# A second group of the last batch's weights in attention's buffers, and the projection's factors behind their group's last product

## The chip, the core and the metric

The kernel runs on one core of a Trainium2 chip. Its time is device microseconds of one execution, of which the median of three runs is given. The engines are called as in the profile: PE is the matrix engine (PEld its weight loads), DVE the vector engine, ACT the scalar engine, POOL the general engine, SP the one that here only issues transfers. Each engine takes its instructions in its own order; an instruction whose input or output buffer is not ready holds up all behind it on that engine.

## The reference

Sliding-window attention with a distance bias, then a maxout layer with an output projection, all in float32. Cut to what is computed:

```python
# q, k, v: 8 batches x 8 heads x 576 positions x 64
scores = scale * np.matmul(q, k.transpose(0, 1, 3, 2))
bias = slopes[:, None, None] * (-np.abs(rel).astype(np.float32))[None, :, :]
mask = (rel >= 0) & (rel < window)            # window = 128
scores = np.where(mask, scores + bias[None], -1000000000.0)
scores = scores - np.max(scores, axis=-1, keepdims=True)
attn = np.exp(scores)
attn = attn / (np.sum(attn, axis=-1, keepdims=True) + 1e-09)
out = np.matmul(attn, v)
# x: the heads side by side, 4608 tokens x 512; w1, w2, w3: 512 x 768; w_out: 768 x 512
h = np.maximum(np.maximum(x @ w1, x @ w2), x @ w3)
return h @ w_out
```

## The kernel before, in words

**Two pipelines in one program.** For each of the eight batches there is attention (four head pairs, 36 steps of 128 queries or less) and then the maxout layer. Attention of batch b+1 runs between the maxout products of batch b. The last batch has no attention to run beside it.

**The maxout layer by units.** A batch's layer is 11 groups of 7 products, 77 *units*. Groups 0 to 8 are the gates: three blocks p of hidden features, and for each block the three weight matrices w = 0, 1, 2, so that p and w are the group's number divided by 3 and the rest. Groups 9 and 10 are the output projection. A group computes four quarters of a tile from seven half-size products (a Strassen scheme: seven products of sums and differences of quarters in place of eight), and each float32 product is made of three products of a high and a low part. So one gate product is 6 matmuls of 128x128 weights with 288 columns, and a group is 42. The seven products stand in the order k = 0, 1, (6 of the group before), 2, 3, 4, 5. Three of PSUM's banks (`ps_m0` to `ps_m2`) take turns: k = 0, 1 and 4 open one each, the others add to an open one. ACT copies the sums after k = 0, 1, 2 aside (L663), and `put` (L596) takes each finished quarter out of its bank: on DVE with L617/L618 or L612 where it is compared with the maximum so far, L620 and ACT's L614 for the first of the three matrices. The last quarter, (1, 0), comes from k = 6, so its take-out (L612) is in the middle of the next group, and the bank that it frees is the one that the next group's k = 4 opens.

**The factors of the projection.** When the third matrix of a block is done, the block's four quarters (`hq`) are the projection's input, and `factors_h` (L562) makes the seven factors from them: differences on DVE (`sub`, L531), and for each factor a high part on ACT (L527) and a low part on DVE (L528), into `hs`. They are put on a list with a unit's number (`later`, L519), and a unit first calls what is due by its number. For the blocks p = 0 and 1 the factors are needed only in groups 9 and 10, for p = 2 right away.

**The weights.** The nine gate groups' factors are made once, in the first batch, and kept in HBM (`keep`, two halves for each group: k = 0 to 3, 1024 KB, and k = 4 to 6, 768 KB). From then on each group's halves are loaded again by transfers that POOL issues (`stream`, L273, one call in each unit), into a ring of two tiles for each half (`wt`). A half is loaded when the product that reads it last in the group two before has been issued. In the last batch group 2 goes elsewhere: `SPARE` is its number in the whole run, and `spare` (L230) loads its seven pieces into buffers that attention no longer needs, as soon as the last batch's layer has begun (`begun == B`). The groups after it then find the ring free one group earlier.

**What sets the order.** All calls are sorted by a time written out by hand (`at`, L672), in steps of attention. The framework's scheduler then orders each engine's instructions by its own estimate; from the third batch of attention on, PE is held to the written order (`fix`).

```python
 ps = part_of[n, {2: 0, 5: 0, 6: 0, 3: 1}.get(k, k)]
 if w == 2:
     factors_h(b, p, ij, when + 1)
```

Of the kernel before, what the change touches and what calls it, by code (L numbers as in the profile page):

```python
# [24 lines left out]
RING = 2  # L25
# [7 lines left out]
def attention_maxout_kernel(  # L33
# [11 lines left out]
    nc = tc.nc  # L45
# [177 lines left out]
    SPARE = 9 * (B - 1) + 2  # L223

    def ahead(n, a):
        if n == SPARE:
            return begun == B
        return n < RING or (n - RING - (SPARE < n <= SPARE + RING), 6 if a else 3) in used

    def spare(n, a):  # L230
        for k in range(4 - a):
            w = (pp_p if a == 0 else s_p if k < 2 else v_p).tile(
                [P, 2, W], F32R, name="pp" if a == 0 else "pr" if k < 2 else "v", **({"bufs": 2} if a and k < 2 else {})
            )
            nc.gpsimd.dma_start(w, keep[n % 9][a][:, k])
            wts[n, a, k] = w

# [35 lines left out]
    def stream():  # L273
        nonlocal streamed
        n, a = divmod(streamed, 2)
        if n < 9 * B and prepared == 72 and ahead(n, a):
            streamed += 1
            if n == SPARE:
                return spare(n, a)
            place(n, a)  # L280
            nc.gpsimd.dma_start(wts[n, a], keep[n % 9][a])  # L281
# [237 lines left out]
    def later(when, what, *args):  # L519
        todo.append((when, what, args))  # L520
        todo.sort(key=lambda x: x[0])
# [40 lines left out]
    def factors_h(b, p, ij, when):  # L562
        b00, b01, b10, b11 = [hq.get((p, x)) for x in ((0, 0), (0, 1), (1, 0), (1, 1))]

# [11 lines left out]
        if ij == (0, 0):  # L576
# [3 lines left out]
            later(when, cut, 0, b00)  # L580
            later(when, cut, 1, t)
        elif ij == (1, 1):
            t = hq["t2", p]
            later(when, sub, t, b11, hq["t1", p])
            later(when, sub, b01, b11, b01)
            later(when, cut, 2, t)
            later(when, cut, 3, b11)
        elif ij == (1, 0):
            t = hq["t2", p]
            later(when, cut, 5, b01)  # L590
            later(when, cut, 4, b10)
            when += 2
            later(when, sub, t, b10, t)
            later(when, cut, 6, t)
# [31 lines left out]
    def unit(u):  # L626
# [9 lines left out]
        if g < 9:  # L636
            at = b * 9 + g
            if b == 0:
                weights(1.3, 6 * g_order.index(g) + 3 + (2, 2, 3, 3, 1, 2, 1)[k])
            wt, x = wts[at, k // 4][:, k % 4] if at != SPARE else wts[at, k // 4, k % 4], xs[b, k]  # L640
            pairs = [
                (wt[:, a, kt * P:(kt + 1) * P], x[:, c, kt]) for kt in range(2) for a, c in ((0, 1), (1, 0), (0, 0))
# [135 lines left out]
```

## Time and profile before

| what | value |
|---|---|
| time, median of 3 runs | 781.05 us (779.34 to 781.97) |
| profiled execution | 781.4 us, of which the span of its instructions 779.7 us |
| PE busy | 750.3 us, 96% of the span |
| DVE busy | 554.6 us, 71% |
| ACT busy | 520.8 us, 67% |
| POOL busy | 188.1 us, 24% |
| read from HBM, written | 157.74 MB, 25.95 MB |

A group's row in the profile has the line, the engine, the operation, the tile written and the tiles read, the shape and the count, then busy time and the mean of one. In a table of waits a row says which engine sat idle at which line, for whose work it waited, the sum, the number of times and the longest. In a timeline a row has start, length, engine, line, tiles and count, and in brackets the idle time before it with what ended it. Line numbers are those of the kernel before.

### The profile page before, as it was taken

How to read it: one execution, taken by the hardware profiler on the slowest of the kernel's cores; microseconds unless marked ns; L12 is line 12 of the kernel's file. 1: busy time of each engine (PE TensorE's matmuls, PEld its weight loads, DVE VectorE, ACT ScalarE, POOL GpSimd, SP SyncE). 2: the span in 40 equal slices, each digit the busy share in tenths (PEclk: the TensorE clock that was granted, in tenths of full speed). 3: DMA queues.
4: the chain of work that ended last, by engine and by line, in shares of the span. 5: the costliest groups of instructions: out<-in, count | busy, mean ns of one | idle time of the engine just before them, and what ended most of it. 6: DMA issues, size and time to landing. Idle time of an engine off the chain costs nothing.

```text
span 779.7 us, 19483 instructions
## 1 busy us (share of the span) xinstructions
PE 750.3 (96%) x7291; PEld 684.6 (88%) x7291; DVE 554.6 (71%) x1722; ACT 520.8 (67%) x1684; POOL 188.1 (24%) x393
## 2 busy tenths in 40 slices
PE   7888999999999999999999999999999999999997
PEld 3556878889998999999999998999999998999987
DVE  5888889885767847694777747794777747683662
ACT  6898787776767756776677766776677666542341
POOL 5331223211232122221222122221222122421100
PEclk9999999999999999999999999999999999999999
DMA  6862668594887559873888568974887567876651
GB/s 243 300 248 73 252 236 322 199 305 140 275 311 264 174 199 297 299 275 125 278 295 282 172 217 290 307 258 136 284 290 272 170 229 261 282 268 201 225 173 61
DMA packets 42398, 184.95 MB, mean 237 GB/s; under 512 B 4672, under 2 KB 13632, under 8 KB 33216
## 3 DMA queue, kind: packets, MB, share of 16 engines
q0 software_dynamic: 18864, 115.61, 44.1%
q1 hardware_dynamic: 23296, 67.97, 24.5%
q8 instruction: 57, 0.93, 0.5%
q14 instruction: 37, 0.30, 0.1%
q10 hardware_dynamic: 144, 0.13, 0.1%
HBM read 157.74 MB, written 25.95 MB: 236 GB/s over the span
## 4 chain that ended last, share of the span: by engine, by line
PE 64%; DVE 16%; ACT 8%; issue 7%; DMA 3%; POOL 1%; SPq 0%; POOLq 0%; DVEq 0%; ACTq 0%
PE ps_m L654 47%; PE ps_s L345 4%; PE pt L413 4%; PE ps_x L480 4%; DVE hs L528 3%; ACT p L386 2%; DVE hq L618 2%; DVE t L617 2%; PE pt L191 2%; DVE t L531 2%; DMA qk<-in_qk 1%; DMA hs<-in_w_all 1%; PE ps_m L191 1%; DMA wt<-keep 1%; DVE s L374 1%
## 5 line engine op out<-in xcount | busy, mean ns | idle before, releaser
L654 PE MATMUL ps_m<-xs,wt 128*128 128x288 f32 x2982 | 425.0, 298 | 10.4 <-DVE hq L612 3.6
L654 PEld LDWEIGHTS ps_m<-xs,wt 128*128 128x128 f32 x2982 | 402.8, 189 | 18.0 <-DVE hq L612 5.2
L663 ACT COPY t<-ps_m 128x288 f32<-128x288 f32 x264 | 103.3, 395 | 81.7 <-PE ps_m L654 79.0
L654 PE MATMUL ps_m<-hs,ow 128*128 128x288 f32 x1008 | 141.1, 297 | 3.4 <-DVE hs L528 1.6
L654 PEld LDWEIGHTS ps_m<-hs,ow 128*128 128x128 f32 x1008 | 134.4, 188 | 6.5 <-ACT t L663 2.6
L433 POOL TENSOR_SCALAR_AFFINE_SELECT pp<-pr 128x256 f32<-128x256 f32 x112 | 54.2, 484 | 313.1 <-ACT pr L417 183.2
L386 ACT ACTIVATE p<-s,st 128x128 f32<-128x128 f32 x288 | 115.1, 403 | 17.2 <-DVE st L374 14.5
L281 POOL DMA_DIRECT2D wt<-keep x124 | 66.9, 539 | 205.2 <-PE ps_m L654 199.5
L405 ACT ACTIVATE p<-p,st 128x128 f32<-128x128 f32 x252 | 85.4, 395 | 23.8 <-DVE st L393 23.5
L617 DVE TENSOR_TENSOR t<-ps_m,t 128x288 f32<-128x288 f32 x144 | 64.9, 453 | 48.1 <-PE ps_m L654 30.2
L374 DVE CUSTOM_DVE_ANT_0 s<-ps_s,bias 128x128 f32<-128x128 f32 x240 | 60.9, 286 | 11.8 <-POOL bias L116 4.7
L618 DVE TENSOR_TENSOR hq<-t,hq 128x288 f32<-128x288 f32 x144 | 65.5, 460 | 2.6
L345 PE MATMUL ps_s<-qk 64*64 64x192 f32 (+1 forms) x1088 | 63.4, 317 | 2.1 <-DMA qk<-in_qk 1.4
L527 ACT CAST hs<-hq 128x288 fp32r<-128x288 f32 x96 | 41.1, 434 | 23.3 <-DVE hq L618 20.6
L386 ACT ACTIVATION_READ_ACCUMULATOR p<-s,st 128x1 f32 x288 | 56.0, 195 | 0.0
L480 PE MATMUL ps_x<-pp,v 64*64 64x64 f32 (+3 forms) x1456 | 55.2, 274 | 0.0
L514 DVE TENSOR_TENSOR xk<-ps_x,xk 128x256 f32<-128x256 f32 (+3 forms) x56 | 25.5, 454 | 41.8 <-ACT xk L513 41.8
L480 PEld LDWEIGHTS ps_x<-pp,v 64*64 64x64 f32 x1456 | 42.3, 133 | 10.8 <-issue 9.2
L413 PE MATMUL pt<-plus,p 128*128 128x128 f32 x288 | 47.5, 286 | 1.5 <-POOL p L400 0.6
L437 POOL TENSOR_SCALAR_AFFINE_SELECT pp<-pr 128x256 f32<-128x256 f32 (+1 forms) x112 | 48.6, 434 | 1.1
L345 PEld LDWEIGHTS ps_s<-qk 64*64 64x64 f32 x1088 | 40.0, 134 | 9.3 <-issue 3.9
L413 PEld LDWEIGHTS pt<-plus,p 128*128 128x128 f32 x288 | 30.2, 140 | 19.8 <-issue 12.6
(98 smaller groups left out, 816.2 us busy)
## 6 DMA issues: line engine op xcount, KB each, us to landing
wt<-keep POOLq DMA_DIRECT2D x62, 1024.0 KB, 7.3
wt<-keep POOLq DMA_DIRECT2D x62, 768.0 KB, 5.9
qk<-in_qk SPq DMA_DIRECT2D x31, 576.0 KB, 5.3
hs<-in_w_all SPq DMA_DIRECT2D x12, 1023.6 KB, 7.0
v<-in_v SPq DMA_DIRECT2D x32, 320.0 KB, 5.8
keep<-wt SPq DMA_DIRECT2D x9, 1024.0 KB, 5.6
outT<-t SPq DMA_DIRECT2D x64, 144.0 KB, 1.8
keep<-wt SPq DMA_DIRECT2D x9, 768.0 KB, 4.6
```

The costliest lines, as they stand in the source:

```text
L281: nc.gpsimd.dma_start(wts[n, a], keep[n % 9][a])
L345: pe(nc.tensor.matmul(ps[j][d:d + D, o:o + k1 - k0], lhsT=qkt[u][j * D:(j + 1) * D, 0, q0:q0 + D], rhs=qkt[u][j * D:(j + 1) * D, 1, k0:k1] ...
L374: nc.vector.tensor_tensor_reduce(out=x, in0=ps[j][:, P:2 * P], in1=below, scale=-0.125, scalar=3.0e38, op0=ALU.add, op1=ALU.min, accum_out ...
L386: nc.scalar.activation(p[:, j], x, AF.Exp, bias=st[:, 0, a, j:j + 1], scale=-1.0, accum_out=st[:, 1, a, j:j + 1])
L405: nc.scalar.activation(p[:, j], p[:, j], AF.Copy, scale=st[:, 2, a, j:j + 1])
L413: pe(nc.tensor.transpose(out=pt[:, a, j], in_=p[:, j], identity=ident))
L433: nc.gpsimd.affine_select(out=old, in_=src, pattern=[[-x, n] for x, n in pat], compare_op=ALU.is_gt, fill=0.0, base=0, channel_multiplier=1,)
L480: pe(nc.tensor.matmul(x[j * D:(j + 1) * D, r, o:o + rhs.shape[1]], lhsT=vv[k, i, j * D:(j + 1) * D], rhs=rhs[k], start=start, stop=True, s ...
L617: nc.vector.tensor_tensor(out=s, in0=ps, in1=e, op=ALU.add)
L618: nc.vector.tensor_tensor(out=h, in0=s, in1=h, op=ALU.max)
L654: pe(nc.tensor.matmul(ps, lhsT=lt, rhs=rt, start=i == 0 and k in (0, 1, 4), stop=i == len(pairs) - 1, skip_group_check=True,))
L663: nc.scalar.copy(out=e, in_=ps)
```

## The change

Three things are changed.

`SPARE` becomes a list of two groups, 2 and 3 of the last batch. Group 3's first half goes into the two buffers of attention's queries and keys (`qk`, 512 KB each, two pieces in each), its second half into four buffers of probabilities (`p`, 128 KB each, two for a piece) and one of values (`v`). `spare` issues 9 transfers for it instead of 2. The groups after them go into the ring, group 4 where group 0 was and group 5 where group 1 was.

A weight piece is read through a small function, since one of them now lies in two tiles.

In `factors_h`, for p = 0 and 1 (`late`), everything that was put on the list at the units right behind the quarter is put 3 to 6 units later, so that it is called only after the unit with the group's last product. The one difference that is made at once (`sub(t, b01, b00)`) stays.

```diff
-    SPARE = 9 * (B - 1) + 2
+    SPARE = [9 * (B - 1) + 2, 9 * (B - 1) + 3]
 
     def ahead(n, a):
-        if n == SPARE:
+        if n in SPARE:
             return begun == B
-        return n < RING or (n - RING - (SPARE < n <= SPARE + RING), 6 if a else 3) in used
+        return n < RING or (n - RING - 2 * (SPARE[-1] < n <= SPARE[-1] + RING), 6 if a else 3) in used
 
     def spare(n, a):
+        def tile(pool, name, *shape, **kw):
+            return pool.tile([P, *shape, W], F32R, name=name, **kw)
+
         for k in range(4 - a):
-            w = (pp_p if a == 0 else s_p if k < 2 else v_p).tile(
-                [P, 2, W], F32R, name="pp" if a == 0 else "pr" if k < 2 else "v", **({"bufs": 2} if a and k < 2 else {})
-            )
+            if n == SPARE[0]:
+                w = (
+                    tile(pp_p, "pp", 2) if a == 0 else tile(s_p, "pr", 2, bufs=2) if k < 2 else tile(v_p, "v", 2)
+                )
+            elif a == 0:
+                if k % 2 == 0:
+                    pair = tile(qk_p, "qk", 2, 2)
+                w = pair[:, k % 2]
+            elif k < 2:
+                w = tile(s_p, "p", bufs=4), tile(s_p, "p", bufs=4)
+                for c in range(2):
+                    nc.gpsimd.dma_start(w[c], keep[n % 9][a][:, k, c])
+                wts[n, a, k] = lambda c, m, w=w: w[c][:, m]
+                continue
+            else:
+                w = tile(v_p, "v", 2)
             nc.gpsimd.dma_start(w, keep[n % 9][a][:, k])
-            wts[n, a, k] = w
-
+            wts[n, a, k] = lambda c, m, w=w: w[:, c, m]
...
     def factors_h(b, p, ij, when):
         b00, b01, b10, b11 = [hq.get((p, x)) for x in ((0, 0), (0, 1), (1, 0), (1, 1))]
+        late = p < 2
...
             sub(t, b01, b00)
-            later(when, cut, 0, b00)
-            later(when, cut, 1, t)
+            later(when + 4 * late, cut, 0, b00)
+            later(when + 4 * late, cut, 1, t)
         elif ij == (1, 1):
             t = hq["t2", p]
-            later(when, sub, t, b11, hq["t1", p])
-            later(when, sub, b01, b11, b01)
-            later(when, cut, 2, t)
-            later(when, cut, 3, b11)
+            later(when + 4 * late, sub, t, b11, hq["t1", p])
+            later(when + 5 * late, sub, b01, b11, b01)
+            later(when + 5 * late, cut, 2, t)
+            later(when + 6 * late, cut, 3, b11)
         elif ij == (1, 0):
             t = hq["t2", p]
-            later(when, cut, 5, b01)
-            later(when, cut, 4, b10)
-            when += 2
+            later(when + 4 * late, cut, 5, b01)
+            later(when + 4 * late, cut, 4, b10)
+            when += 2 + 3 * late
             later(when, sub, t, b10, t)
             later(when, cut, 6, t)
```

**DVE, third gate group of a middle batch (p = 0, w = 2).** The order before, from the difference that is made at once (`t_5774`, read by the second factor) to the take-out of the last quarter (L612 from `ps_m_5670`) and the first take-out of the next group (L620). The two `ISA` rows are one score of attention and the read-out of its maximum.

```order
L531 TENSOR_TENSOR t_5774<-hq 128x288
L528 TENSOR_TENSOR hs<-hq,hs 128x288
L531 TENSOR_TENSOR t_5775<-hq,t_5774 128x288
L528 TENSOR_TENSOR hs<-t_5774,hs 128x288
L531 TENSOR_TENSOR hq<-hq 128x288
L528 TENSOR_TENSOR hs<-t_5775,hs 128x288
L528 TENSOR_TENSOR hs<-hq,hs 128x288
L374 ISA s,st<-ps_s,bias_t 128x128
L374 ISA st 128x1
L612 TENSOR_TENSOR hq<-ps_m_5670,hq 128x288
L528 TENSOR_TENSOR hs<-hq,hs 128x288
L620 TENSOR_TENSOR hq<-ps_m_5816,t 128x288
```

The same place with the change (L546 is the line of the differences, L543 that of the low parts, L628 the take-out, L636 the next group's):

```order
L546 TENSOR_TENSOR t_5774<-hq 128x288
L389 ISA s,st<-ps_s,bias_t 128x128
L389 ISA st 128x1
L543 TENSOR_TENSOR hs<-hq,hs 128x288
L546 TENSOR_TENSOR t_5775<-hq,t_5774 128x288
L628 TENSOR_TENSOR hq<-ps_m_5670,hq 128x288
L543 TENSOR_TENSOR hs<-t_5774,hs 128x288
L546 TENSOR_TENSOR hq<-hq 128x288
L543 TENSOR_TENSOR hs<-t_5775,hs 128x288
L636 TENSOR_TENSOR hq<-ps_m_5802,t 128x288
```

Behind the first row there stood eight rows ahead of the take-out, now there stand four; the score has moved up, and three low parts and a difference have moved behind the take-out.

**POOL, attention of the last batch.** With the change the first pair of transfers into a buffer of queries and keys stands between a load into the ring and the two masks (L448, L452) that attention's next product needs (`keep_0_129` is the first half of group 3):

```order
L296 DMA wt_9751<-keep_0_129 128x2048
L296 DMA wt_9811<-keep_1_130 128x1536
L251 DMA qk<-keep_0_129 128x512 x2
L448 AFFINE_SELECT pp<-pr 128x2x128
L452 AFFINE_SELECT pp<-pr 128x2x128
L296 DMA wt_9871<-keep_0_131 128x2048
```

The second pair stands the same way ahead of two later pairs of masks. The rest of the second spare group, three of the four small transfers and the one into `v`, stands behind the first spare group's last piece (`pr`), ahead of the load of group 4:

```order
L296 DMA wt_10594<-keep_1_126 128x1536
L251 DMA pr<-keep_1_128 128x512
L246 DMA p<-keep_1_130 128x256 x3
L251 DMA v<-keep_1_130 128x512
L296 DMA wt_10829<-keep_0_131 128x2048
L296 DMA wt_10874<-keep_1_132 128x1536
```

Before, the load of group 3's first half into the ring followed `pr` directly. PE's order is the same before and after but for the first batch, where the scheduler sets it, and there products of weight preparation (L191), of attention and of the gates have changed places along some 110 rows.

More of the change, by code (lines that the diff above doesn't have):

```diff
@@ L277, in stream @@
             streamed += 1
-            if n == SPARE:
+            if n in SPARE:
                 return spare(n, a)
@@ L639, in unit @@
                 weights(1.3, 6 * g_order.index(g) + 3 + (2, 2, 3, 3, 1, 2, 1)[k])
-            wt, x = wts[at, k // 4][:, k % 4] if at != SPARE else wts[at, k // 4, k % 4], xs[b, k]
+            x = xs[b, k]
+            wt = wts[at, k // 4, k % 4] if at in SPARE else lambda a, m: wts[at, k // 4][:, k % 4, a, m]
             pairs = [
-                (wt[:, a, kt * P:(kt + 1) * P], x[:, c, kt]) for kt in range(2) for a, c in ((0, 1), (1, 0), (0, 0))
+                (wt(a, slice(kt * P, (kt + 1) * P)), x[:, c, kt]) for kt in range(2) for a, c in ((0, 1), (1, 0), (0, 0))
             ]
```

## The prediction

> **What bounds the kernel now.** I read the page's first part, then a table by stretches of the span, then the waits, then the timeline where the waits point.
>
> ```profile
> PE 750.3 (96%) x7291; PEld 684.6 (88%) x7291; DVE 554.6 (71%) x1722; ACT 520.8 (67%) x1684; POOL 188.1 (24%) x393
> ```
>
> PE bounds the kernel; only its idle time can be won, 29.4 us of 779.7. Where that lies is in the table by stretches (length, then busy time of PE, PEld, DVE, ACT, POOL, then granted clock, DMA share, GB/s): the thick of the first batch's weight preparation, a middle batch, and the last batch.
>
> ```profile
> 110.00:160.00 50.00, 46.26 (x460) 40.82 (x459) 43.41 (x114) 36.92 (x105) 13.04 (x20) 1.00 0.68 248
> 438.70:525.40 86.70, 85.86 (x894) 80.97 (x893) 61.68 (x205) 60.07 (x204) 20.99 (x46) 1.00 0.74 248
> 698.80:779.70 80.90, 74.38 (x551) 73.04 (x549) 38.09 (x94) 24.44 (x62) 6.36 (x12) 1.00 0.49 161
> ```
>
> A middle batch has 0.84 us of idle PE in 86.7, the last one 6.5, the 50 us in the first batch 3.74. PE's own waits, first between 178.6 and 698.8 us, then from 698.8 us on:
>
> ```profile
> PE ps_m L654 <- DVE hq L612: 3.6, 6, 0.6
> PE ps_m L654 <- DVE hs L528: 0.6, 2, 0.3
> PE ps_m L654 <- ACT t L663: 0.5, 2, 0.3
> ...
> PE ps_m L654 <- DVE t L531: 1.1, 1, 1.1
> PE ps_m L654 <- DVE hs L528: 0.7, 1, 0.7
> PE ps_m L654 <- DMA wt<-keep: 0.6, 1, 0.6
> PE ps_m L654 <- DVE t L603: 0.6, 1, 0.6
> ```
>
> Two things are there to be won: six waits on the take-out L612, and, in the last batch, waits on loads.
>
> **The factors.** One of the six waits, in the timeline:
>
> ```profile
> 468.71 5.76 PE L654 MATMUL ps_m<-xs,wt 128*128 128x288 f32 x42
> 471.62 0.45 DVE L531 TENSOR_TENSOR t<-hq 128x288 f32<-128x288 f32 x1
> 472.07 0.46 DVE L528 TENSOR_TENSOR hs<-hq,hs 128x288 fp32r<-128x288 f32 x1
> 472.45 0.45 DVE L531 TENSOR_TENSOR t<-hq,t 128x288 f32<-128x288 f32 x1
> 472.87 0.46 DVE L528 TENSOR_TENSOR hs<-t,hs 128x288 fp32r<-128x288 f32 x1
> 474.36 0.28 DVE L374 CUSTOM_DVE_ANT_0 s<-ps_s,bias_t 128x128 f32<-128x128 f32 x1
> 474.56 0.45 DVE L612 TENSOR_TENSOR hq<-ps_m,hq 128x288 f32<-128x288 f32 x1
> 475.07 1.06 PE L654 MATMUL ps_m<-xs,wt 128*128 128x288 f32 x6 [0.60 <-DVE hq L612]
> ```
>
> The row of 42 matmuls is seven products of (5.76 - 0.16) / 7 = 0.80 us, where 0.16 is what the last matmul hangs over. The product that waits (k = 4) opens the bank of k = 6, which is the fifth of the seven and ends at 474.47 - 2 x 0.80 = 472.87. So the data of L612 is there at 472.87, and L612 starts at 474.56: for 1.7 us it stands behind factors and a score that nobody needs yet. In the new order there stand behind the first difference only the score (0.20 from start to start in the rows), one low part (0.38) and one difference (0.42): L612 starts at 471.62 + 0.45 + 0.20 + 0.38 + 0.42 = 473.07 and ends at 473.52, against 475.01 now. It is 1.5 us earlier and PE's wait of 0.60 goes, with 0.9 us to spare. Five batches have this wait at this place and one has it at the next block's factors (0.57), where the order puts the take-out forward by as much. Term: 5 x 0.60 + 0.57 = **3.6 us** won.
>
> What is late next: three low parts and a difference, 4 x 0.45 = 1.8 us of DVE, now stand behind the take-out. The next take-out, L620, which began at 475.30 (two rows behind L612), has three of them before it and not one: 473.52 + 3 x 0.40 = 474.7, still earlier than now. The factors themselves are wanted in group 9, three groups later or more. ACT's copies aside (L663) keep their places among the high parts within one instruction of 0.43 us. One buffer comes free later: there are 7 `hq` tiles, so the next block's fourth quarter (L614 on ACT) takes the first quarter's, whose last reader, the low part of k = 5, moves from 6 units before it to 2. Two units are 1.6 us where nothing but products runs and over 2 beside attention, and DVE's backlog in the rows is about 1.7, so L614 could wait a few tenths; PE is two products away from it. I put this at nothing; without that cover, at 0.3 in each of 16 blocks, it costs 4.8 us. Both ends for this part: 3.6 won, and 3.6 - 4.8, so 1.2 lost.
>
> **The first batch** is ordered by the scheduler, and the moved factors change that order on PE too. What it does to the 3.74 us of idle PE there the trace can't tell: they are waits of this kind,
>
> ```profile
> PE pt L191 <- ACT pr L417: 1.7, 2, 1.4
> PE ps_m L654 <- ACT wt L180: 1.1, 1, 1.1
> PE ps_m L654 <- DVE hq L620: 0.3, 1, 0.3
> PE pt L191 <- ACT pp L422: 0.3, 1, 0.3
> PE pt L191 <- DVE wt L181: 0.3, 1, 0.3
> ```
>
> made by the order in which ACT and DVE get to weights, attention and quarters. DVE has 43.41 of 50 us there, and the same instructions remain. I take 0, with ends of 3.7 won and 3.7 lost (as many such waits again).
>
> **The second spare group.** In the last batch PE takes a group in 42 matmuls, 5.6 us, and POOL's loads (start, length of the issue) and PE's two gaps are:
>
> ```profile
> 729.18 0.53 POOL L281 DMA_DIRECT2D wt<-keep  x1 [3.47 <-PE ps_m L654]
> 730.78 0.53 POOL L281 DMA_DIRECT2D wt<-keep  x1 [1.07 <-PE ps_m L654]
> 735.05 0.53 POOL L281 DMA_DIRECT2D wt<-keep  x1 [3.74 <-PE ps_m L654]
> 736.39 0.53 POOL L281 DMA_DIRECT2D wt<-keep  x1 [0.81 <-PE ps_m L654]
> 743.29 0.53 POOL L281 DMA_DIRECT2D wt<-keep  x1 [1.07 <-PE ps_m L654]
> ...
> 738.77 11.71 PE L654 MATMUL ps_m<-xs,wt 128*128 128x288 f32 x84 [1.08 <-DVE t L531]
> 751.07 5.83 PE L654 MATMUL ps_m<-xs,wt 128*128 128x288 f32 x42 [0.59 <-DMA wt<-keep]
> ```
>
> Time to landing of the first halves issued at 725.18, 730.78, 736.39 and 743.29, each asked for alone:
>
> ```profile
> wt<-keep POOLq DMA_DIRECT2D x1, 1024.0 KB, 5.0
> wt<-keep POOLq DMA_DIRECT2D x1, 1024.0 KB, 7.8
> wt<-keep POOLq DMA_DIRECT2D x1, 1024.0 KB, 7.1
> wt<-keep POOLq DMA_DIRECT2D x1, 1024.0 KB, 7.6
> ```
>
> The gap at 738.77 is put down to a difference on DVE, but group 6's first half, issued at 730.78, lands at 738.6: both gaps are loads. A first half takes 5.0 us alone and 7.1 to 7.8 us when a second half was issued 1.3 to 1.6 us before it, and between issue and need lie 6.9 us (730.78 to 737.69). With the change groups 4 and 5 load where groups 3 and 4 did, before 725, and group 6's first half still starts at 730.8 (it goes where group 4 was, and PE reads group 4 no earlier), but no second half is in front: it lands at 735.8, and the 1.08 goes. Group 7's first half is then what group 6's was: issued at 736.4 behind group 6's second half, it lands at 743.5 to 744.2, where PE wants it at 737.7 + 5.6 = 743.3. That is 0.2 to 0.9 of wait; if it is the smaller, group 8 waits again (7.6 against 6.9 + 0.2, so 0.5). Together some 0.9 is left of 1.67: **0.8 us** won. Ends: 0 (the waits only move) and 1.7 (none is left).
>
> The Trainium skill, in DMA: Bandwidth & Descriptors, section Anatomy of one DMA, puts a transfer issued by POOL at about 2.0 us plus its bytes over 436 GB/s. By that estimate a first half takes 4.4 us, and both halves back to back 6.2, less than the 6.9 there is: no wait on loads would be left, and the sum would be 0.9 us lower. The 5.0 alone is near that; the 7.1 to 7.8 of this trace contradicts it, and I go by the rows.
>
> What the loads cost elsewhere. In attention's last steps POOL's order now has two transfers into `qk` ahead of masks, twice. They wait for the last products that read the buffer:
>
> ```profile
> 640.32 0.82 PE L345 MATMUL ps_s<-qk 64*64 64x192 f32 x14
> 660.04 0.82 PE L345 MATMUL ps_s<-qk 64*64 64x192 f32 x14
> ...
> 634.64 1.08 POOL L281 DMA_DIRECT2D wt<-keep  x2
> 642.26 0.41 POOL L433 TENSOR_SCALAR_AFFINE_SELECT pp<-pr 128x256 f32<-128x256 f32 x1 [2.67 <-ACT pr L425]
> 662.20 0.40 POOL L433 TENSOR_SCALAR_AFFINE_SELECT pp<-pr 128x256 f32<-128x256 f32 x1 [4.48 <-ACT pr L417]
> 649.70 0.90 PE L480 MATMUL ps_x<-pp,v 64*64 64x192 f32 x28
> ```
>
> 641.14 + 1.08 for two issues is 642.2, and the masks start at 642.26; 660.86 + 1.08 is 661.9, against 662.20. PE wants the first masks only at 649.70, so even some 6 us of lateness would be hidden. POOL's other new issues, 5 x 0.54 us, lie before 708, where it sits idle for 17 us. The 1.8 MB more before 700 us is no more in all, only earlier. Cost: nothing.
>
> **The sum**, on the profiled execution's own time: 781.4 - 3.6 - 0.8 = 777.0. The median is 0.35 us below that execution, so **776.7 us**, with 775.2 to 778.2 as the forecast's own range (the 0.8 between its ends, a third of the 3.6 missed or a few more small waits gone).
>
> **Rivals.**
> 1. *The first batch loses.* The order there is a new one, in the stretch where DVE and ACT have the least room; as many waits again, +3.7: 780.4. For it: the last column of nearly every wait there is another engine's order. Against: the factors that move out of the way are the only work there that is not urgent.
> 2. *The wait passes on.* The take-out is early, but the moved low parts hold up L620 or L614 by as much. Then only the loads' 0.8 is won, 780.3, and with all of L614's 4.8 it is 777.0 + 4.8 - 0.35 = 781.5; I put it at 780.6. Against: the sums of start times above leave 0.9 us.
> 3. *Slower.* In the first batch DVE is the engine that is full (43.41 of 50 us). For p = 0 and 1 ten instructions each (seven low parts, three differences) of 0.45 us are put up to 6 units later, into weight preparation, and all of them fall on the path: 2 x 10 x 0.45 = 9.0, 785.7. It comes out slower from 6.7 us of these 9.0 on.
> 4. *The first batch gains* its 3.7 us, because weights no longer stand behind factors: 773.0.
>
> **How the numbers follow.** Forecast 0.60; rivals 0.13, 0.10, 0.07 and 0.10. What a measurement can't tell from no change is 0.3%, 2.3 us: 778.7 to 783.4. Forecast and rival 4 are faster: 0.70; rivals 1 and 2 the same: 0.23; rival 3 slower: 0.07. The range leaves out rival 3, half of rival 4 and a little of 1: 773.8 to 780.4.
>
> **What would show it.** Right: no row of PE waiting for the take-out of the (1, 0) quarter between 178.6 and the end of attention, and a middle batch in 86.1 us for 86.7; in the last batch group 6 starts without a gap, and one gap of up to 1 us stands at group 7 or 8; PE reads `qk` and `p` without waiting; the masks of the last steps are on time. Wrong: PE waits for L620's or L614's line in its place, or POOL's masks start later and PE waits for them. The first batch's idle PE between 110 and 160 us, 3.74 now, decides between the forecast and rivals 1, 3 and 4.

## The result

Over 11 runs of each, side by side, the changed kernel has a median of 777.54 us (776.41 to 780.38) and the kernel before 781.05 us (778.46 to 786.92): a ratio of 0.995, 95% interval 0.9927 to 0.9973. That is 3.5 us, with an interval of 2.1 to 5.7. The forecast was 776.7. The profiled execution took 776.49 us, 4.9 below the profiled one of before, of which 1.4 is where the two lie among their runs: the one 0.35 above its median, the other 1.05 below.

Much of the spread goes with the TensorE clock granted in a run. Of the changed kernel's 11 runs, the five with a mean granted clock of 0.998 took 776.41 to 776.95 us and the six with 0.992 to 0.995 took 777.54 to 780.38. Of 35 runs of the kernel before, made beside the experiments with the two parts, the 12 with 0.997 or more have a median of 778.70 us and the nine with 0.993 or less one of 782.71. In the profiled executions there are stretches of 3.41 us in which the clock is halved: each of them has one that begins at 68 to 72 us, four have another that begins at 12 to 14 us, and two have another at 141 us; the one that begins at 772 us or later stands behind PE's last product.

Line numbers of the changed kernel: products L671 (before L654), the take-out of the last quarter L628 (L612), the first matrix's take-out L636 (L620), the factors' high parts L542, low parts L543, differences L546, ACT's copies aside L680, loads into the ring L296. First the page's busy times and the table by stretches (length, busy PE, PEld, DVE, ACT, POOL, clock, DMA share, GB/s):

```profile
PE 748.1 (97%) x7286; PEld 684.4 (88%) x7291; DVE 556.1 (72%) x1722; ACT 517.0 (67%) x1684; POOL 193.3 (25%) x400
```

```profile
110.00:160.00 50.00, 46.61 (x467) 42.02 (x466) 44.21 (x119) 38.31 (x113) 12.92 (x23) 1.00 0.69 249
438.70:525.40 86.70, 86.25 (x897) 81.38 (x896) 62.31 (x208) 59.66 (x207) 21.73 (x48) 1.00 0.74 248
698.80:774.80 76.00, 70.09 (x522) 69.18 (x520) 37.56 (x92) 23.44 (x60) 5.28 (x10) 1.00 0.43 145
```

PE still bounds it, now with 26.7 us idle in place of 29.4. In the same 50 us of the first batch 3.39 us are idle (3.74 before), and in the window of a middle batch 0.45 (0.84). PE's waits, from 178.6 to 698.8 us and then from 698.8 us on:

```profile
PE ps_m L671 <- DVE hq L636: 0.9, 5, 0.2
...
PE ps_m L671 <- DMA wt<-keep: 0.6, 1, 0.6
...
PE ps_m L671 <- DMA wt<-keep: 1.1, 1, 1.1
```

All six waits on the last quarter's take-out are gone. In the place that the prediction shows, the take-out now starts at 469.53, 1.3 us behind the first difference (468.21), where it was 2.9 behind it (474.56 and 471.62); 1.45 was forecast. What is left out of the table are waits that were there before and one of 0.3. There are two new entries: five small ones on the next take-out (L636), and one on a load before the last batch, at 675.92. In the timeline of PE the loads' waits are these:

```profile
675.92 5.83 PE L671 MATMUL ps_m<-xs,wt 128*128 128x288 f32 x42 [0.56 <-DMA wt<-keep]
...
716.88 1.76 PE L671 MATMUL ps_m<-xs,qk 128*128 128x288 f32 x12
...
720.88 1.76 PE L671 MATMUL ps_m<-xs,p 128*128 128x288 f32 x12
...
724.88 14.56 PE L671 MATMUL ps_m<-xs,wt 128*128 128x288 f32 x108
740.50 11.43 PE L671 MATMUL ps_m<-xs,wt 128*128 128x288 f32 x84 [1.06 <-DMA wt<-keep]
```

PE takes the second spare group out of `qk` and `p` without a wait, group 6 starts inside a row of 108 matmuls without a gap, and one gap of 1.06 is left ahead of group 7. In the last batch the two gaps before were 1.67 together.

**Where the time went.** For the comparisons below I cut each profiled execution at events that every kernel has: the gate product with which PE goes on after a wait on DVE's low part (before, it waits 2.8 us and starts at 69.15; two gate products stand earlier, at 54.85, but the texts here call this one the first), then the last score products of each batch of attention from the third on, then the end of PE's last row. Each number is the distance between two such places in PE's timeline of one execution, in us. "Loads' stretch" is the last scores to that end.

| kernel | first gate product to 3rd batch's scores | to the 4th's | four middle batches | loads' stretch |
|---|---|---|---|---|
| before | 158.75 | 84.89 | 86.73, 86.77, 86.90, 86.73 | 116.19 |
| before again | 158.04 | 84.97 | 86.71, 86.82, 87.07, 86.76 | 115.52 |
| before, third time | 158.15 | 84.91 | 86.99, 86.77, 86.99, 86.77 | 116.04 |
| the change | 157.51 | 83.35 | 86.36, 86.36, 86.85, 86.37 | 115.89 |
| the change again | 157.39 | 83.35 | 86.37, 87.15, 86.68, 86.37 | 115.42 |

The second, third and last rows are single extra executions of unchanged kernels. The fourth batch's stretch repeats within 0.1 us; the first and the last one vary by up to 0.7. In most executions one of the middle batches is 0.2 to 0.8 longer than the others; in those of the change one wait on a load or on DVE stands there. The kernels before and after both have it, at changing places, and no run explains it; the granted clock does not, as it is 1.00 in all of these batches. So a middle batch is read by its commonest value: 86.75 before, 86.37 with the change. What comes ahead of the first gate product is left out: its start varies by 2.5 us from one execution to the next, whatever the change.

### The profile page after: what moved, and what is told of

The parts are those of the page before. It is cut to its first block, busy times and chain, and to the rows that moved or that the text cites. A ratio compares the mean times of both kernels' runs of the same rounds, so it can differ in the third digit from the quotient of the medians.

```text
span 774.8 us, 19484 instructions
## 1 busy us (share of the span) xinstructions
PE 748.1 (97%) x7286; PEld 684.4 (88%) x7291; DVE 556.1 (72%) x1722; ACT 517.0 (67%) x1684; POOL 193.3 (25%) x400
## 4 chain that ended last, share of the span: by engine, by line
PE 57%; DVE 21%; ACT 9%; issue 7%; DMA 4%; POOL 1%; POOLq 0%; DVEq 0%; ACTq 0%
PE ps_m L671 41%; DVE hs L543 4%; PE ps_s L360 4%; PE pt L428 4%; PE ps_x L495 3%; DMA wt<-keep 3%; DVE hq L634 3%; DVE t L633 3%; ACT p L401 2%; DVE t L546 2%; ACT p L420 2%; PE pt L191 2%; DVE s L389 1%; DVE xk L529 1%; PE pt L304 1%
## 5 line engine op out<-in xcount | busy, mean ns | idle before, releaser
L671 PE MATMUL ps_m<-xs,wt 128*128 128x288 f32 x2940 | 417.9, 298 | 6.5 <-DVE xs L543 2.8
L671 PEld LDWEIGHTS ps_m<-xs,wt 128*128 128x128 f32 x2940 | 396.9, 189 | 12.8 <-ACT t L680 3.3
L680 ACT COPY t<-ps_m 128x288 f32<-128x288 f32 x264 | 103.0, 393 | 77.4 <-PE ps_m L671 74.9
L671 PE MATMUL ps_m<-hs,ow 128*128 128x288 f32 x1008 | 141.1, 297 | 3.4 <-DVE hs L543 1.7
L671 PEld LDWEIGHTS ps_m<-hs,ow 128*128 128x128 f32 x1008 | 134.5, 188 | 6.5 <-DVE hs L543 2.6
L448 POOL TENSOR_SCALAR_AFFINE_SELECT pp<-pr 128x256 f32<-128x256 f32 x112 | 53.8, 480 | 296.4 <-ACT pr L432 175.7
L296 POOL DMA_DIRECT2D wt<-keep x122 | 65.6, 538 | 200.1 <-PE ps_m L671 194.5
L542 ACT CAST hs<-hq 128x288 fp32r<-128x288 f32 x96 | 40.3, 433 | 21.7 <-DVE hq L634 20.5
L452 POOL TENSOR_SCALAR_AFFINE_SELECT pp<-pr 128x256 f32<-128x256 f32 (+1 forms) x112 | 51.7, 462 | 1.1
```

The lines of the kernel that those rows point to most:

```text
L448: nc.gpsimd.affine_select(out=old, in_=src, pattern=[[-x, n] for x, n in pat], compare_op=ALU.is_gt, fill=0.0, base=0, channel_multiplier=1,)
L671: pe(nc.tensor.matmul(ps, lhsT=lt, rhs=rt, start=i == 0 and k in (0, 1, 4), stop=i == len(pairs) - 1, skip_group_check=True,))
L680: nc.scalar.copy(out=e, in_=ps)
```

## The experiments

**Each part alone.** The factors alone are the kernel before with the new list of factors:

```diff
     def factors_h(b, p, ij, when):
         b00, b01, b10, b11 = [hq.get((p, x)) for x in ((0, 0), (0, 1), (1, 0), (1, 1))]
+        late = p < 2
...
-            later(when, cut, 0, b00)
+            later(when + 4 * late, cut, 0, b00)
```

> The later factors alone, one spare group as before. Theory A (the later factors bring nearly all): the six waits on the (1, 0) take-out go, a middle batch is 86.35 us for 86.71 as in the changed kernel, the first batch ends about 1 us earlier, the group 6 and group 8 waits on loads of the last batch stay at 1.08 and 0.59, and no wait on a load shows before 690 us: 4 to 4.5 us under the kernel before, ratio 0.994 to 0.996. Rival B (the two parts share the gain): 2 us under, ratio 0.9975, and the first batch unchanged.

Measured over 12 runs: 777.09 us against 780.94, ratio 0.9955 (0.9939 to 0.9971). Part of these 3.85 us is the clock that the runs happened to get: at a mean granted clock of 0.997 or more the medians are 776.38 (7 runs) and 778.70 (12 runs), 2.3 apart, and at 0.992 to 0.995 they are 778.63 (4) and 781.72 (15), 3.1 apart. Stretches: 157.61, 83.58, then 86.32, 86.38, 86.84, 86.68, and 116.02. In PE's timeline the two gaps in the last batch are as before, only exchanged, 1.72 together for 1.67:

```profile
734.17 5.83 PE L655 MATMUL ps_m<-xs,wt 128*128 128x288 f32 x42 [0.55 <-DMA wt<-keep]
...
741.17 11.43 PE L655 MATMUL ps_m<-xs,wt 128*128 128x288 f32 x84 [1.17 <-DMA wt<-keep]
```

The spare group alone is the changed kernel with `late` off:

```diff
-        late = p < 2
+        late = False
```

> The second spare group alone, factors as before. Theory A (what the loads win in the last batch they lose in the batch before it): one wait of about 0.5 us on a load between 670 and 685 us, one wait of about 1.1 us at group 7 of the last batch instead of two at groups 6 and 8, in sum -0.3 to +0.2 us: ratio 0.9995 to 1.0005; the six waits on L612 of 0.6 us stay. Rival B: the last batch gains 0.8 us and nothing is lost, ratio 0.999.

Measured over 12 runs: 779.94 us, ratio 1.0004 (0.9983 to 1.0024). Stretches: 158.36, 84.89, then 86.77, 86.73, 86.89, 86.74, and 115.08. The six waits are all there, in PE's table of waits:

```profile
PE ps_m L671 <- DVE hq L628: 3.6, 6, 0.6
```

Its loads' stretch is 0.84 shorter than the mean of the three executions of before (115.92) and 0.44 shorter than the shortest of them; 0.8 was forecast. The last batch has one gap, 0.62, and no wait on a load before it. So by the trace rival B holds, and theory A's wait between 670 and 685 us did not come. The times don't show it: 0.8 us is less than their interval of 1.6 us to each side, and each stretch is that of one execution. So nearly all of the change's 3.5 us is the factors; what the spare group wins alone is mostly gone in the full change, where the stretch takes 115.89 and 115.42.

**The load in the batch before.** What takes it away again is the wait at 675.92. In POOL's timeline of the change:

```profile
667.32 0.55 POOL L251 DMA_DIRECT2D v<-keep  x1
667.86 0.54 POOL L296 DMA_DIRECT2D wt<-keep  x1
668.38 0.55 POOL L246 DMA_DIRECT2D p<-keep  x1
```

The second row is the first half of the seventh batch's group 8. It stands between two small transfers into spare buffers, one of 256 KB of the first spare group and one of 128 KB of the second. Its row in the list of transfers, with the time from issue to landing; then, of before, that of the same load (issued at 672.47), and PE's row that takes it up:

```profile
wt<-keep POOLq DMA_DIRECT2D x1, 1024.0 KB, 7.9
```

```profile
wt<-keep POOLq DMA_DIRECT2D x1, 1024.0 KB, 7.0
```

```profile
678.18 7.43 PE L654 MATMUL ps_m<-xs,wt 128*128 128x288 f32 x54
```

667.86 + 7.9 is 675.8, and PE starts at 675.92 after 0.56 of waiting. Before, it landed at 672.47 + 7.0 = 679.5. The row of 54 is two products of group 7 and then group 8, and twelve matmuls of (7.43 - 0.16) / 54 = 0.135 us end at 679.8: some 0.3 us of room, which the trace of before had and the prediction did not look for. From issue to need there are 7.5 us now and 7.3 before; it is the landing that has become longer. In the kernel with the factors alone, which lacks the second group's transfers, the same load lands in 5.1. To test whether they are the cause, the second group's nine transfers are held to the order in which the program writes them, and that puts them behind this load:

```diff
-                    nc.gpsimd.dma_start(w[c], keep[n % 9][a][:, k, c])
+                    tc.keep_in_program_order(nc.gpsimd.dma_start(w[c], keep[n % 9][a][:, k, c]))
...
-            nc.gpsimd.dma_start(w, keep[n % 9][a][:, k])
+            load = nc.gpsimd.dma_start(w, keep[n % 9][a][:, k])
+            if n == SPARE[1]:
+                tc.keep_in_program_order(load)
```

> The whole change, but the nine transfers of the second spare group are pinned on POOL behind everything written before them, so that most of them start after attention's last masks. Theory A (the 0.56 us wait at 675.9 us comes from the loads started at 637, 657, 667 and 668 us, which slow the load of the batch's last group): the wait goes, and the last batch keeps its single wait at group 7: 0.5 to 0.9 us under the changed kernel. Rival (that load is late for POOL's masks ahead of it, as it nearly was before): the wait stays at 0.4 to 0.6.

The load in POOL's timeline and its landing in the list of transfers:

```profile
669.05 0.55 POOL L298 DMA_DIRECT2D wt<-keep  x1
669.59 0.54 POOL L251 DMA_DIRECT2D qk<-keep  x1
```

```profile
wt<-keep POOLq DMA_DIRECT2D x1, 1024.0 KB, 5.8
```

It lands in 5.8 us and PE doesn't wait for it. Which of the moved transfers made it late is not separated: the 256 KB one into `v` still stands ahead, now 2.1 us instead of 0.5, and a 256 KB one into `qk` right behind. The one wait on a load that is left is 0.76 ahead of group 7, and the loads' stretch is 114.85, 1.1 less than before's mean, where the gaps' 1.67 less 0.76 makes 0.9. The time over 12 runs is 777.77, ratio 0.9969 (0.9951 to 0.9988); that is not under the factors alone (777.09), but 0.9 us is not to be seen in times whose interval is 1.5 us to each side. The gain rests on the stretch of this one execution.

**What is left of the gap in the last batch.** The prediction said that group 7's first half lands late because group 6's second half is in front of it. The rows in the change's POOL timeline, and the landing of the first halves issued at 726.94 and 732.55 in the list of transfers:

```profile
726.94 0.53 POOL L296 DMA_DIRECT2D wt<-keep  x1 [12.27 <-PE ps_m L671]
731.21 0.53 POOL L296 DMA_DIRECT2D wt<-keep  x1 [3.74 <-PE ps_m L671]
732.55 0.53 POOL L296 DMA_DIRECT2D wt<-keep  x1 [0.81 <-PE ps_m L671]
```

```profile
wt<-keep POOLq DMA_DIRECT2D x1, 1024.0 KB, 5.0
...
wt<-keep POOLq DMA_DIRECT2D x1, 1024.0 KB, 7.8
```

Group 6's takes 5.0 with nothing in front, group 7's 7.8 with 768 KB issued 1.3 us ahead. 732.55 + 7.8 is 740.4, where PE goes on. The experiment leaves the second halves of groups 6 to 8 of the last batch unloaded, and PE multiplies with group 5's instead:

```diff
+            if n > 9 * (B - 1) + 5 and a:
+                wts[n, a] = wts[9 * (B - 1) + 5, a]
+                return
             place(n, a)
```

> The changed kernel, but in the last batch the second halves of groups 6, 7 and 8 are not loaded: their products k = 4 to 6 read group 5's second half. This leaves out part of the computation, so its time stands for the loads only. Theory A (a first half takes 7.8 us and PE waits 1.06 us at group 7 because a second half was issued just before it): group 7's first half lands 5.0 us after its issue, about 1.7 us before it is wanted, and PE has no wait on a load in the last batch; the time from the last attention product to the end is 1.0 us shorter, 114.9 us for 115.9. Rival B (that half is slow by itself, by where it lies in HBM): it still takes 7 us or more and the wait stays.

Measured: 776.29 us (one execution). Group 7's first half is issued at 733.88, and these are its row in the list of transfers and, from PE's timeline, what became of the gap:

```profile
wt<-keep POOLq DMA_DIRECT2D x1, 1024.0 KB, 5.1
```

```profile
725.95 25.76 PE L674 MATMUL ps_m<-xs,wt 128*128 128x288 f32 x192
```

192 matmuls without a wait, through group 8, and a loads' stretch of 113.80. With no second half in front the landing falls from 7.8 to 5.1: that is the cause of the gap, and not the rate at which these loads run by themselves. The formula of the Trainium skill, DMA: Bandwidth & Descriptors, section Anatomy of one DMA (about 2.0 us plus the bytes over 436 GB/s, so an estimate of 4.4 for a first half alone), is near the 5.0 to 5.2 measured when nothing is in front; its estimate of 6.2 for a second and a first half one behind the other counts from the second half's issue, and from there 740.4 - 731.2 = 9.2 were measured, 3.0 more. The prediction set the 6.2 beside the time from the first half's issue, which is 1.3 us later.

**What a middle batch gives back.** Each wait on the take-out was shown as 0.60, and the weight load's wait with it is longer. The two tables of PEld's waits from 178.6 to 698.8 us, before and with the change:

```profile
PEld ps_m L654 <- DVE hq L612: 5.0, 6, 0.8
PEld ps_m L654 <- ACT t L663: 3.4, 10, 0.6
...
PEld ps_m L654 <- DVE hq L620: 1.7, 5, 0.4
```

```profile
PEld ps_m L671 <- ACT t L680: 4.9, 14, 0.5
...
PEld ps_m L671 <- DVE hq L636: 2.0, 5, 0.4
```

The score products of attention serve as markers, in PE's timeline before and with the change. Between the first two rows lies one of the six waits, between the last two group 5 of the next batch:

```profile
293.19 0.82 PE L345 MATMUL ps_s<-qk 64*64 64x192 f32 x14
303.28 0.74 PE L345 MATMUL ps_s<-qk 64*64 64x128 f32 x16
...
322.13 0.74 PE L345 MATMUL ps_s<-qk 64*64 64x128 f32 x16
331.22 0.33 PE L345 MATMUL ps_s<-qk 64*64 64x192 f32 x2
```

```profile
290.54 0.82 PE L360 MATMUL ps_s<-qk 64*64 64x192 f32 x14
299.77 0.74 PE L360 MATMUL ps_s<-qk 64*64 64x128 f32 x16
...
318.70 0.74 PE L360 MATMUL ps_s<-qk 64*64 64x128 f32 x16
328.19 0.33 PE L360 MATMUL ps_s<-qk 64*64 64x192 f32 x2
```

Across the wait 10.09 us become 9.23: 0.86 are won, about the weight load's 5.0 / 6 = 0.83. But from the third row to the fourth 9.09 become 9.49, 0.40 lost, in group 5, where nothing was forecast. ACT, PEld and DVE there, in the timeline of the change:

```profile
322.70 0.43 ACT L542 CAST hs<-t 128x288 fp32r<-128x288 f32 x1
...
323.95 0.21 ACT L407 ACTIVATE st<-st 128x4 f32<-128x4 f32 x1
324.19 0.18 DVE L408 RECIPROCAL st<-st 128x4 f32<-128x4 f32 x1 [0.19 <-ACT st L407]
324.40 1.28 ACT L420 ACTIVATE p<-p,st 128x128 f32<-128x128 f32 x4 [0.24 <-DVE st L408]
325.58 0.67 ACT L680 COPY t<-ps_m 128x288 f32<-128x288 f32 x2
326.01 1.63 PEld L671 LDWEIGHTS ps_m<-xs,wt 128*128 128x128 f32 x12 [0.33 <-ACT t L680]
```

The last factor's high part (0.43) has been moved in among attention's exponentials. The instruction that finishes the sums of the softmax rows (L407), their reciprocal, the four normalisations and the copy aside behind them are all 0.4 later, measured from the score products just before (reciprocal 5.09 us behind them before, 5.49 now; copy 6.49 and 6.88). Of the 0.40, 0.06 are there before the high part: the exponentials themselves start 2.34 us behind the scores before and 2.40 now. PE waits for that copy, which frees a bank. To test it, the last difference is called three units later still and its high part is held to its written place on ACT:

```diff
+        high = nc.scalar.copy(out=hi, in_=src)
+        if pin:
+            tc.keep_in_program_order(high)
...
-            split((t[:, 0], t[:, 1]), src, nc.vector)
+            split((t[:, 0], t[:, 1]), src, nc.vector, late and k == 6)
...
-            when += 2 + 3 * late
+            when += 2 + 6 * late
```

> The whole change, but the last difference and the last factor of p = 0 and 1 come 3 units later still, and its high part on ACT is pinned behind what is written before it, which puts it behind the normalising of attention's probabilities. Theory A (in each middle batch the 0.47 us given back come from that high part standing between exponentials on ACT, which makes the reciprocal, the normalising and the copy of a sum 0.4 us late): PE's weight loads no longer wait 0.3 us for that copy in group 6, and a middle batch takes 85.9 to 86.1 us for 86.35: 1 to 2 us under the changed kernel over five batches. Rival B (they come from the low parts on DVE ahead of the next take-outs): 86.35 stays. This also changes the first batch's order, by an unknown amount of up to 1.5 us.

ACT and PEld in the same group, one batch later:

```profile
411.13 4.82 PEld L673 LDWEIGHTS ps_m<-xs,wt 128*128 128x128 f32 x36 [0.30 <-ACT t L682]
...
412.72 1.28 ACT L420 ACTIVATE p<-p,st 128x128 f32<-128x128 f32 x4 [0.25 <-DVE st L408]
413.91 0.67 ACT L682 COPY t<-ps_m 128x288 f32<-128x288 f32 x2
...
415.73 0.44 ACT L542 CAST hs<-t 128x288 fp32r<-128x288 f32 x1
```

The edit also moves the last difference and the low part on DVE; what points at the high part is that the wait ended with ACT's copy. The high part comes behind normalising and copy, PEld's wait of 0.33 is gone (36 loads in one row), and middle batches take 86.04, 86.94, 86.04, 86.05: in the common value 0.33 less than with the change and 0.7 less than before (the 86.94 has a wait of 0.7 on a load). The other stretches are 157.68, 83.49 and 115.83. The time over 12 runs is 777.87, ratio 0.9965 (0.9942 to 0.9988): 4 x 0.33 = 1.3 us is plain in the trace's stretches and less than the times' interval of 1.8 to each side.

**The first batch.** It was forecast at nothing, between 3.7 won and 3.7 lost. One kernel keeps the old list of factors there:

```diff
-        late = p < 2
+        late = p < 2 and b > 0
```

> The whole change, but in the first batch the factors stay where they were. Theory A (some 1.2 us of the gain are the first batch's, because take-outs and weights no longer stand behind factors there): from the first gate product to the third batch's attention 158.4 us, as with the second spare group alone, for 157.5 with the whole change; the middle batches as in the changed kernel, 86.36. Rival B (that gain is a new order by chance and any change of it brings it): 157.5 or less here too.

Measured: 776.83 us (one execution), stretches 157.30, 83.35, then 86.38, 86.33, 86.74, 86.35, and 115.90. The first stretch is no longer than the change's 157.51. Beside all the other executions that have the same order of instructions on PE there (on DVE and ACT the order differs in three places at most, all in the second batch): with before's order 157.30 to 158.75 (five, mean 158.1), with the change's 156.87 to 158.00 (six, mean 157.4). Some 0.7 us may be won; the two overlap by 0.7, so that is not settled. No execution of the change's order shows a loss there.

**Both mends together**, transfers held and high part pinned:

> The whole change with the second spare group's transfers held back as in the run with held transfers, and the last factor pinned as in the run with the pinned cast. Theory: the two do not touch: middle batches of 86.04 us, and 114.9 us from the last attention product to the end: 2.2 us under the changed kernel, 775.3 us, ratio to the kernel before 0.9925 to 0.993. Rival: the pinned cast moves DVE's low part into the last steps of attention and a wait of 0.5 us comes back there: 775.9.

Measured over 9 runs: 776.31 us against 780.33, ratio 0.9933 (0.9907 to 0.9959); 775.3 was forecast. Middle batches 86.37, 86.18, 86.64, 86.04, loads' stretch 114.82; but the first stretch is 159.02. Pinning the high part changes the first batch's order too, and this order has 157.68, 159.02 and 159.47 in three executions, the second and third of them here and in the next kernel. The order is not what sets them apart: it is the same in all three on PE, DVE and ACT. In the second and the third the granted clock is halved at 141 us. Five us at this place, in the first execution and then in the second, by the table by stretches and by PE's timeline:

```profile
142.00:147.00 5.00, 4.55 (x36) 4.32 (x34) 4.91 (x12) 2.83 (x12) 1.11 (x2) 1.00 0.11 42
143.77 2.56 PE L673 MATMUL ps_m<-xs,wt 128*128 128x288 f32 x18
```

```profile
140.00:145.00 5.00, 4.55 (x24) 4.31 (x23) 4.08 (x10) 2.01 (x8) 0.94 (x2) 0.66 0.02 5
142.23 3.45 PE L675 MATMUL ps_m<-xs,wt 128*128 128x288 f32 x18
```

PE is busy for 4.55 us in both, but does 24 matmuls where it did 36, and the same three gate products take 3.45 us instead of 2.56; where the clock is halved, their matmuls start every 0.24 us instead of 0.133. Counted from the first gate product, the second execution is 0.16 us ahead of the first at this place and 1.37 behind it 3.7 us later, a loss of 1.53; in the third it is 1.27. Without them the pinned order takes 157.7, 157.5 and 158.2, where the change's order takes 156.9 to 158.0.

**A version that takes the last gap too.** When PE has read groups 2 and 3 of the last batch out of attention's buffers, groups 6 and 7 go into the same buffers, so that the ring has two groups fewer to take. Both mends are kept.

```diff
-    SPARE = [9 * (B - 1) + 2, 9 * (B - 1) + 3]
+    SPARE = [9 * (B - 1) + g for g in (2, 3, 6, 7)]
...
-            return begun == B
-        return n < RING or (n - RING - 2 * (SPARE[-1] < n <= SPARE[-1] + RING), 6 if a else 3) in used
+            return begun == B and (n in SPARE[:2] or (n - 4, 6 if a else 3) in used)
+        return n < RING or (n - RING - 2 * (n > SPARE[1]), 6 if a else 3) in used
...
-            if n == SPARE[0]:
+            if n in SPARE[::2]:
```

> As the held and pinned kernel, and groups 6 and 7 of the last batch go into the buffers of the spare groups 2 and 3 as these come free, so that group 8 goes where group 4 was in the ring. Theory A (the wait at group 7 is a load that starts too late for its turn in the ring): no wait on a load in the last batch, another 0.8 to 1.06 us less than held and pinned, about 774.4 us. Rival B (the transfers' rate in the last batch is the bound, 285 GB/s against the 320 wanted): a wait of 0.5 us or more stays at group 7 or 8.

Measured over 6 runs: 774.99 us (774.80 to 776.25) against 780.33, ratio 0.992 (0.989 to 0.9949); 774.4 was forecast. In PE's timeline group 6 begins out of `pp`, and no row of the last batch's gates has a wait:

```profile
725.10 8.96 PE L675 MATMUL ps_m<-xs,wt 128*128 128x288 f32 x66
733.90 1.76 PE L675 MATMUL ps_m<-xs,pp 128*128 128x288 f32 x12
```

Stretches: 159.47, 83.83, then 86.00, 86.02, 85.99, 86.05, and 113.79. The loads' stretch is 2.1 less than before's and equal to that without the second halves (113.80), so nothing is left there for a load to win. The first stretch has the 1.27 us of halved clock. The last kernel leaves the first batch unpinned, on the reading that its order was the shorter one:

```diff
-            split((t[:, 0], t[:, 1]), src, nc.vector, late and k == 6)
+            split((t[:, 0], t[:, 1]), src, nc.vector, late and k == 6 and b > 0)
...
-            when += 2 + 6 * late
+            when += 2 + (6 if b else 3) * late
```

> As the kernel with reused buffers, but in the first batch the last factor is where the change put it, so that the first batch has the changed kernel's order and not the pinned one. Theory: the first batch up to the third batch's attention takes 157.3 us (mean of the four runs with that order) for 159.2 with the pinned order, the rest is as with reused buffers (86.0 a middle batch, 113.8 at the end): 1.9 us under the kernel with reused buffers, 773.1 us, ratio to the kernel before 0.990. Rival (the 159.2 are chance): 775.

Measured over 6 runs: 774.94 us against 779.95, ratio 0.9933 (0.991 to 0.9956). Stretches: 158.00, 83.13, then 86.88, 85.99, 86.04, 86.49, and 113.77. The forecast of 773.1 is missed and the rival holds: the 159.2 were chance, namely the clock halved at 141 us, which this execution does not have. So its first stretch is 1.5 shorter than that of the kernel just before, and the median of the runs is the same. Two middle batches have the unexplained extra waits. These two are the fastest kernels of this study, 5.3 and 5.0 us under the runs of the kernel before beside them, where the change was 3.5 under its own.

**The spread.** Three unchanged kernels, one execution each, for the table in the section on the result:

> The kernel before once more, for how much the first batch varies with one and the same order. Theory A (the new order saves the first batch 0.8 us): 158.1 plus or minus 0.7 from the first gate product to the third batch's attention, as in the three runs with this order (158.75, 158.36, 157.30). Rival B (no difference between the orders): 157.4 or less.

> The kernel before a second time more, with the same expectations: theory A 158.1 plus or minus 0.7 from the first gate product to the third batch's attention, rival B 157.4 or less.

> The changed kernel once more. Theory A: 157.3 plus or minus 0.4 from the first gate product to the third batch's attention, as in the four runs with this order (157.51, 157.61, 157.24, 156.87), one wait of 0.2 to 0.6 us on a load between 670 and 685 us and one of 0.8 to 1.1 at group 7. Rival B (no difference between the orders): 158 or more.

780.74, 780.75 and 776.48 us. The first stretches, 158.04, 158.15 and 157.39, lie where theory A put them; with 157.30 for before's order in the run above that does not settle it. The six waits, 3.6 us, are in before's again and not in the change's. The load at 675.92 costs 0.2 there in place of 0.56, so that loss is real but varies.

## Why the prediction was right, and where its terms were not

The time, 777.5 for 776.7, came out of terms that were partly wrong and partly cancelled, so that it came this close is partly luck. Measured from the stretches: factors 3.1 (1.54 in the fourth batch's stretch with two waits, and four middle batches at 0.4), spare group about 0.3 (115.92 to the mean of 115.89 and 115.42), first batch perhaps 0.7: together 4.1, against 3.5 between the medians, whose interval is 2.1 to 5.7.

- **The factors, forecast 3.6, measured 3.1.** The mechanism was right: the take-out's data had been there long before, it moved ahead of the work that nobody waited for, and all six waits are gone. Two sizes were off, in opposite directions. The step "5 x 0.60 + 0.57" took PE's shown wait. The whole delay is that of the weight load, 0.83 each, and 6 x 0.83 is 5.0 us. The step "ACT's copies aside (L663) keep their places among the high parts within one instruction of 0.43 us" was true and was wrongly read as free: one instruction of 0.43 on ACT, in group 5, made up most of the 0.40 that each middle batch lost there, since the sums, reciprocal, normalisation and copy behind it were just on time. Moving it brought back 0.33 (86.37 to 86.04). So a middle batch took 86.37, and not the 86.1 named as the sign of being right.
- **L620 and L614.** The step that gave L620 three low parts ahead of it and called it "still earlier than now" was nearly right: PEld's waits for it went from 1.7 to 2.0 over the five, 0.3 in all. PE's table shows it as five new waits, 0.9 in all, which the prediction had named as a sign of being wrong; by the weight loads it is a third of that. No wait on L614's line came.
- **The spare group, forecast 0.8, measured 0.8 alone and about 0.3 in the change.** In the last batch the steps held: group 6's gap went, group 7's became 1.06, and 0.8 in the repeat (forecast 0.2 to 0.9), and it came from the second half in front. What failed is "The 1.8 MB more before 700 us is no more in all, only earlier. Cost: nothing." The prediction checked the masks, which were on time, and did not ask which other load in POOL's order has little room. Group 8's in the batch before had about 0.3 us.
- **The first batch, forecast nothing.** Idle PE in its window went from 3.74 to 3.39, and the first stretch from a mean of 158.1 to one of 157.4, with overlap; some tenths are won at most, well inside the ends. Neither the rival that loses 3.7 there, nor the slower one, nor the one that gains 3.7 has happened.
- **The wait that passes on** took place in small: hardly to L620 (0.07 a batch) and not to L614, where the rival put it, but to a copy on ACT, and for about half of what each middle batch won (0.40 of 0.83).

## What to carry to other kernels

A wait at a matmul cost here what the weight load waited, so read PEld's table beside PE's before pricing it. When instructions that nobody waits for are moved, look at each engine that they land on for a chain that is just on time there: ask of every place by how much the next needed result is early, not whether the moved work is small. The same holds for a queue of transfers: loads that were brought forward were paid for here by the load with the least room, one batch before the one that they were for. And before a longer stretch is put down to a new order of instructions, look at the clock granted in it: here 1.5 us of it were read as an order, and a kernel was built on that.

## What the runs showed of the hardware

- A transfer of 1024 KB took 5.0 to 5.2 us when nothing was in front of it and 7.8 with one of 768 KB issued 1.3 us ahead; leaving that one out made it 5.1. One with 256 KB issued 0.5 us ahead and 128 KB 0.5 us behind, and others of the second spare group before, took 7.9; it took 5.1 in the kernel without that group and 5.8 with that group issued behind it.
- PE's shown wait of 0.60 went with a delay of 0.83 to 0.86 us of all that follows.
- One instruction of 0.43 us on ACT, busy 67% of the span, delayed PE by 0.33 in each middle batch.
- In two executions the granted clock was halved for 3.41 us in the thick of the first batch: the matmuls of a gate product started every 0.24 us instead of 0.133, and all that follows came 1.3 to 1.5 us later. The time of a run went with its mean granted clock: medians of 778.70 and 782.71 us for runs of one kernel at 0.997 or more and at 0.993 or less.
- The start of the first gate product moved between 68.4 and 70.9 us in the executions seen, as much as most effects in this study. The landing of attention's first load does not explain it, at 3.9 to 4.1 us in all. The three latest (70.5 to 70.9) have the clock halved at 12 to 14 us, but so has one that starts at 69.1, and the cause is open.
